# A scan layer and an MLP on one core: the state's part of y moved, PSUM banks named, the transposes of C and B taken apart

## The chip, the core and the metric

The kernel runs on one core of a Trainium2 chip. The metric is the device time of one execution in microseconds (us). The kernel before was run four times: 368.15, 368.38, 367.01 and 365.83 us, a median of 367.58. Engines are named as in the profile: PE (TensorE's matmuls), PEld (TensorE's weight loads), DVE (VectorE), ACT (ScalarE), POOL (GpSimd), and SP, whose queue issues all transfers.

## What is computed

Two layers, one after the other, for 4 batches, 8 heads, 768 tokens, head width D = 32, state width N = 16. The first is a scan in chunks (the reference takes chunks of 32 tokens; the result does not depend on the length):

```python
cum = np.cumsum(la, axis=-1)                      # la = log of the decay a, within a chunk
L = np.exp(cum[:, :, :, None] - cum[:, :, None, :]) * causal
M = np.einsum('bhin,bhjn->bhij', Cc, Bc) * L      # scores, decayed
y_intra = np.einsum('bhij,bhjd->bhid', M, xc)     # own products
y_inter = np.einsum('bhin,bhnd->bhid', Cc, state) * decay_to_i[:, :, :, None]
y[:, :, sl] = y_intra + y_inter
state = decay_full * state + np.sum(Bx, axis=2)
```

The second is an MLP on the 3072 tokens: `h = x @ w_in` (256 to 2048), `g = h * clip(h + 3, 0, 6) / 6`, `out = g @ w_out` (2048 to 256). The weights arrive as 64-bit floats, and DVE and ACT decode them to fp32 at the start.

## The kernel before

**Tiling.** The kernel works in NC = 6 chunks of 128 tokens, all 4 batches together, and each chunk in two halves of 64 tokens. Every engine's instructions stand in the order in which the code is written out by hand (`manual_schedule`); waits between engines follow from the tiles. Chunk c of the scan is computed while the MLP of chunk c - 1 runs; the main loop is over k, the MLP's chunk, with c = k + 1.

**The scan for a chunk.** `load_bc` and `load_x` bring C, B and x (L85, L112). The decays L come from `diff_mask`, `diff_less`, `diff_pick` and `diff_exp` for chunks 0 and 1 (L309 to L340: a bank is filled with a mask by one matmul, then sums of logs are added, then ACT takes exp), and by a transfer through DRAM with `conceal` and `decay` for later ones. `turn(c, p)` (L389) transposes C and B for two batches at a time on TensorE into one bank t_ps; ACT copies bT, and ACT or DVE make cT (C masked for odd and even heads) and csT (C times the decay from the chunk's start, eto). From chunk 3 on `turn_all` does this on DVE. `scores(c)` (L433) makes the products cb of B and C in four banks and the sums sp for the state in banks y0 and y1, then on DVE multiplies L by cb (L463) and forms mid, later and the new state (L469 to L485). `mix(c)` (L492) then makes y in four banks: one blank product (L503), the state's products for both halves (L510; mid for second halves, the last chunk's state for first halves), then the own products (L519). `keep` copies y to SBUF as yT by four ACT copies, `sum_y` forms differences of its quarters.

**The MLP.** For k = 0, `mlp_in` (L534) makes each of 16 blocks h by plain products into bank tag "f", ACT takes the ramp, DVE multiplies (L618), and the decoding of the weights is woven between (`weights(i, n)` takes n more steps of part i; parts 0 to 3 are w_in, 4 to 7 are w_out). `first_out` makes the output, and between its calls the scan of chunk 1 is called: turn, scores, results. For k >= 1, both products run by a scheme with seven half products in place of eight: `lead`, `early`, `middle` and `last` (L582 to L609) for 8 steps s, `out_units` (L676) for the output; in it, scores(c) stands at unit 2 and results(c), which is mix, keep and sum_y, at unit 6. For k = 1 the calls turn(2, 0) and turn(2, 1) stand at steps 3 and 5.

**Banks.** PSUM has 8 banks: pool ps with four buffers under the one tag "f", taken in turn, ps_o with two, and ps_y with y0 and y1.

**The start.** Before the first h: masks for chunks 0 and 1, logs and their sums, diff for chunk 0, decoding of part 0, diff for chunk 1, eto, `ends` (POOL: B times decay), turn(0, 0) and turn(0, 1), scores(0), mix(0), `by_token` (four transposes into c_ps, L300, and one DVE step), keep(0), and the rest of part 1:

```python
diff_exp(1, 2)
diff_exp(1, 3)
weights(1, 1)
scores(0)
ys = mix(0)
by_token()
keep(0, ys)
weights(1, 4)
```

Of the kernel before, what the change touches and what calls it, by code (L numbers as in the profile page):

```python
# [20 lines left out]
def kernel(  # L21
# [45 lines left out]
    ps = ctx.enter_context(tc.tile_pool(name="ps", bufs=4, space=PSUM))  # L67
# [229 lines left out]
    def by_token():  # L297
        c_ps = ps.tile([P, NC, G], FP32, name="c_ps", tag="f")
        for c in range(2, NC):
            nc.tensor.transpose(out=c_ps[:, c], in_=cum_c[:, c], identity=ident[:G, :G])  # L300
        nc.vector.tensor_scalar(
            out=cum_n[:, 2:], in0=c_ps[:, 2:], scalar1=-1.0, scalar2=None, op0=ALU.mult)


    yTs, states, mids, bTs, bss, tmps = {}, {}, {}, {}, {}, {}

    ds = {}

    def diff_mask(c, b):  # L309

        if c == 0:
            d = ps.tile([P, NH, HT], FP32, name="d", tag="f")
        elif b < 2:
            d = ps_o.tile([P, NH, HT], FP32, name="d", tag="o")
        else:
            d = ps_y.tile([P, NH, HT], FP32, name="d", tag=f"y{b % 2}")
        nc.tensor.matmul(
            out=d, lhsT=ident_h, rhs=hide.unsqueeze(1).to_broadcast([P, NH, HT]),
            start=True, stop=True)
        ds[c, b] = d  # L320
# [21 lines left out]
    def first_eto():  # L342

        e_ps = ps.tile([P, NB, HT], FP32, name="e_ps", tag="f")
        for b in range(NB):
            nc.tensor.matmul(
                out=e_ps[:, b],
                lhsT=picks[:, b * P:(b + 1) * P],
                rhs=split[:, 0, HALF[1]], start=(b == 0), stop=True, skip_group_check=True)
        etos[0] = att.tile([P, NB, P], FP32, name="eto")  # L350
        nc.scalar.activation(etos[0][:, :, HALF[1]], e_ps, AF.Exp)
# [37 lines left out]
    def turn(c, p):  # L389


        bT, cT, csT = turned(c)
        bs_ = slice(2 * p, 2 * p + 2)
        pool, tag = (ps, "f") if c < 2 else (ps_o, "o")
        t_ps = pool.tile([P, 4, P], FP32, name="t_ps", tag=tag)
        for k in range(4):
            j, b = k // 2, 2 * p + k % 2
            nc.tensor.transpose(  # L398
                out=t_ps[:, k],
                in_=bcs[c][j][:, b * NH:(b + 1) * NH].rearrange("s h n -> s (h n)"),  # L400
                identity=ident)
        nc.scalar.copy(out=bT[:, bs_], in_=t_ps[:, 2:4])
        if c == 1 and p == 0:
            from_start(c)
            carry(c)
            for b in range(NB):
                ends(c, b)
        if c == 1 or (c, p) == (0, 1):
            for t in range(2):
                nc.scalar.activation(  # L410
                    cT[:, bs_, t], t_ps[:, 0:2], AF.Copy, scale=parity[:, t:t + 1])
        else:
            nc.vector.tensor_tensor(
                out=cT[:, bs_], in0=t_ps[:, 0:2].unsqueeze(2).to_broadcast([P, 2, 2, P]),
                in1=parity.unsqueeze(1).unsqueeze(3).to_broadcast([P, 2, 2, P]), op=ALU.mult)
        sl = slice(0, P) if c else HALF[1]
        nc.vector.tensor_tensor(
            out=csT[:, bs_, sl], in0=t_ps[:, 0:2, sl], in1=etos[c][:, bs_, sl], op=ALU.mult)
# [13 lines left out]

    def scores(c):  # L433


        bT, cT, _ = bTs[c]
        L, xt, bs = Ls[c], xts[c], bss[c]
        cbs = [ps.tile([P, NB, 2, HT], FP32, name="cb", tag="f") for q in range(NQ)]
        for b in range(NB):
            for a, rows in enumerate(HALF):  # L440
                for q in range(NQ):
                    pair = slice(32 * q, 32 * q + 32)

                    nc.tensor.matmul(  # L444
                        out=cbs[q][rows, b], lhsT=bT[pair, b, rows], rhs=cT[pair, b, :, rows],
                        start=(b == 0), stop=True, tile_position=(32 * q, a * HT),
                        skip_group_check=True)
        halves = range(2 if c < NC - 1 else 1)
        sps = [ps_y.tile([P, NB, 2 * D], FP32, name=f"sp{a}", tag=f"y{a}") for a in halves]
        for b in range(NB):  # L450
            for q in range(NQ):
                hs = slice(b * NH + 2 * q, b * NH + 2 * q + 2)
                for a in halves:
                    nc.tensor.matmul(  # L454
                        out=sps[a][32 * q:32 * q + 32, b],
                        lhsT=bs[HALF[a], hs].rearrange("s h n -> s (h n)"),
                        rhs=xt[HALF[a], hs].rearrange("s h d -> s (h d)"),
                        start=True, stop=True, tile_position=(a * HT, 32 * q),
                        skip_group_check=True)

        def pair_decayed(q):
            hs = slice(2 * q, 2 * q + 2)
            nc.vector.tensor_tensor(  # L463
                out=L[:, :, hs], in0=L[:, :, hs], in1=cbs[q], op=ALU.mult)

        def new_state(t, sp, old):
            for u in range(2):
                ds_ = slice(u * D, (u + 1) * D)
                nc.vector.scalar_tensor_tensor(  # L469
                    out=t[:, :, ds_], in0=sp[:, :, ds_], scalar=parity[:, u:u + 1],  # L470
                    in1=old[:, :, ds_], op0=ALU.mult, op1=ALU.add)

        pair_decayed(0)
        mids[c] = mid = att.tile([P, NB, 2 * D], FP32, name="mid", bufs=1)
        if c:
            new_state(mid, sps[0], tmps[c])
        else:
            nc.vector.tensor_tensor(
                out=mid.rearrange("p b (t d) -> p b t d", t=2),
                in0=sps[0].rearrange("p b (t d) -> p b t d", t=2),  # L480
                in1=parity.unsqueeze(1).unsqueeze(3).to_broadcast([P, NB, 2, D]), op=ALU.mult)
        if c < NC - 1:
            states[c] = att.tile([P, NB, 2 * D], FP32, name="state")
            later = att.tile([P, NB, 2 * D], FP32, name="later", bufs=1)
            nc.vector.tensor_tensor(  # L485
                out=later, in0=mid, in1=etos[c][:, :, P - 1:P].to_broadcast([P, NB, 2 * D]),
                op=ALU.mult)
            new_state(states[c], sps[1], later)
        for q in range(1, NQ):
            pair_decayed(q)  # L490

    def mix(c):  # L492

        xt, csT = xts[c], bTs[c][2]
        ys = {(a, 0): ps_y.tile([P, NB, HT], FP32, name=f"y{a}", tag=f"y{a}") for a in range(2)}
        for a in range(2):
            y2 = ps.tile([P, 2, NB, HT], FP32, name="y2", tag="f")
            ys[a, 1] = y2[:, 0]  # L500


        nc.tensor.matmul(  # L503
            out=y2[:, 1], lhsT=ident_h, rhs=hide.unsqueeze(1).to_broadcast([P, NB, HT]),
            start=True, stop=True, skip_group_check=True)
        for b in range(NB):
            for a in range(0 if c else 1, 2):
                for q in range(NQ):
                    pair, d0, u = slice(32 * q, 32 * q + 32), 2 * D * (q % 2), q // 2
                    nc.tensor.matmul(  # L510
                        out=ys[a, u][d0:d0 + 2 * D, b],
                        lhsT=(mids[c] if a else states[c - 1])[pair, b],
                        rhs=csT[pair, b, HALF[a]], start=(b == 0 and (a, u) != (1, 1)),
                        stop=True, tile_position=(32 * q, d0), skip_group_check=True)
        for b in range(NB):
            for h in range(NH):
                for a, rows in enumerate(HALF):
                    d0 = D * (h % HU)
                    nc.tensor.matmul(  # L519
                        out=ys[a, h // HU][d0:d0 + D, b], lhsT=xt[rows, b * NH + h],  # L520
                        rhs=Ls[c][rows, b, h], start=(c + a + b == 0), stop=True,
                        tile_position=(a * HT, d0), skip_group_check=True)
        return ys

    def keep(c, ys):

        yTs[c] = att.tile([P, NK, NB, P], FP32, name="yT")
        for (a, u), y in ys.items():
            nc.scalar.copy(out=yTs[c][:, u, :, HALF[a]], in_=y)
# [4 lines left out]
    def mlp_in(k, f):  # L534
        h = ps.tile([P, NK, 2 * P], FP32, name="h", tag="f")
# [46 lines left out]
    def lead(k, s):  # L582
# [3 lines left out]
        pool, tag = (ps, "f") if s % 3 == 2 else (ps_y, f"y{s % 3}")  # L586
        odds[k, s] = odd = pool.tile([P, 2, 2 * P], FP32, name="odd", tag=tag)
        evens[k, s] = even = ps.tile([P, 2, 2 * P], FP32, name="even", tag="f")
# [158 lines left out]
    def results(c):  # L747
        keep(c, mix(c))
# [17 lines left out]
    for c in range(2):  # L766
        for b in range(NB):
            diff_mask(c, b)
# [6 lines left out]
    for part in (diff_less, diff_pick):  # L775
        for b in range(NB):
            part(0, b)
# [9 lines left out]
    weights(0, 2)  # L787
    store_rows()
    for part in (diff_less, diff_pick):
        for b in range(NB):  # L790
            part(1, b)
    first_eto()
    for b in range(NB):
        ends(0, b)
    turn(0, 0)
    turn(0, 1)
    diff_exp(1, 2)
    diff_exp(1, 3)
    weights(1, 1)
    scores(0)  # L800
    ys = mix(0)
    by_token()
    keep(0, ys)
    weights(1, 4)
# [9 lines left out]
    for k in range(NC):  # L814
        gTs[k] = ffn.tile([P, NF, TB], FP32, name="gT")
        c, ahead = k + 1, k + 2
        if k == 0:
# [11 lines left out]
            for i in range(NP):  # L829
                for b in range(NB):  # L830
# [8 lines left out]
                    elif (i, b) == (2, 0):  # L839
                        turn(c, 0)  # L840
                        turn(c, 1)
                        for p in range(2):
                            conceal(ahead, p)
                    elif (i, b) == (2, 1):
                        scores(c)
                        next(sums_in)
# [40 lines left out]
        for i, _ in enumerate(out_units(k)):  # L887
# [8 lines left out]
            if c < NC:  # L896
                if i == 2:
                    scores(c)
                if ahead < NC and 2 <= i < 6:
# [41 lines left out]
```

## Time and profile before

| what | value |
|---|---|
| median of four runs | 367.58 us (365.83 to 368.38) |
| profiled execution, its own time | 368.15 us |
| its span, first to last instruction | 366.4 us |
| its mean granted clock | 0.991 |
| DVE, ACT, POOL busy | 61%, 48%, 37% |
| bytes moved | 24.95 MB, mean 68 GB/s |

The page's first part gives each engine's busy time and its share of the span. The second cuts the span into 40 slices of 9.16 us; a digit is tenths busy, and in the row PEclk tenths of TensorE's full clock. The third lists the transfer queues with packets, MB and share. The fourth follows the chain that ended last back from the end. In the chain in order of time a piece has its start and its length in us, the engine, the tile it writes and the line; "issue" is time in which an engine waited for nothing that the profile shows. In a list of waits a line says who waited for whom: total us, how often, and the longest.

Fp32 products take two passes, so the profile counts twice as many matmuls as the code has (L510 and L519 in chunk 4: 64 and 128, with as many weight loads).

### The profile page before, as it was taken

The page shows a single profiled execution, that of the slowest core. Times are in us where ns is not written, and L with a number is a line of the kernel's source. Part 1 is how long each engine was busy: PE and PEld are TensorE (multiplying, and loading weights), DVE is VectorE, ACT ScalarE, POOL GpSimd, SP SyncE. Part 2 cuts the span into 40 slices and gives each one's busy share as a digit, 9 for nine tenths or more (in the row PEclk, how much of TensorE's full clock was granted, in tenths as well). Part 3 has the DMA queues.
Part 4 walks back from the last instruction along what each step waited for, and adds up shares of the span by engine and source line. Part 5 has one row for each costly group of instructions (what it writes and reads, how often), then busy time and mean ns, then how long its engine had stood idle before and what let it go on. Part 6 is the DMA issues. An engine that isn't in the chain of part 4 may idle for free.

```text
span 366.4 us, 9281 instructions
## 1 busy us (share of the span) xinstructions
PE 351.3 (96%) x3910; PEld 301.0 (82%) x3910; DVE 225.0 (61%) x429; ACT 175.5 (48%) x389; POOL 137.4 (37%) x138
## 2 busy tenths in 40 slices
PE   6769999999999989999989999999999999999996
PEld 2544448878788989888989888999888999888996
DVE  7558999876588616588517488436488412488111
ACT  4738878447575730476640366550366110367100
POOL 3300000172299812069803059910057800058800
PEclk9969999999999999999999999999999999999999
DMA  9967979900936016460007442000000000000000
GB/s 168 168 269 168 124 267 144 161 2 32 184 46 87 4 31 147 73 93 8 2 4 174 65 83 27 2 4 30 29 0 3 2 4 30 30 1 2 0 30 29
DMA packets 78537, 24.95 MB, mean 68 GB/s; under 512 B 69088, under 2 KB 74880, under 8 KB 77984
## 3 DMA queue, kind: packets, MB, share of 16 engines
q1 hardware_dynamic: 78496, 24.37, 35.6%
q8 instruction: 30, 0.49, 0.6%
q14 instruction: 11, 0.09, 0.1%
HBM read 21.07 MB, written 3.29 MB: 66 GB/s over the span
## 4 chain that ended last, share of the span: by engine, by line
PE 93%; DVE 3%; issue 1%; DMA 1%; ACT 1%; DVEq 0%; ACTq 0%
PE even L579 19%; PE ob L688 18%; PE oa L688 17%; PE odd L579 14%; PE h L537 8%; PE o L629 7%; PE y L519 3%; PE cb L444 2%; PE y L510 1%; PE sp L454 1%; PE d L323 1%; PE d L332 1%; DMA out_dram<-ob 1%; PE t_ps L398 1%; DMA pre<-in_a_dram 1%
## 5 line engine op out<-in xcount | busy, mean ns | idle before, releaser
L674 POOL TENSOR_TENSOR s<-gT 128x512 f32<-128x512 f32 x20 | 26.4, 1320 | 88.0 <-DVE gT L618 88.0
L579 PE MATMUL even<-ts,w_sum 128*128 128x256 f32 x160 | 48.2, 383 | 0.0
L592 ACT COPY even<-odd 128x512 f32<-128x512 f32 x40 | 23.0, 575 | 47.1 <-PE odd L579 44.9
L613 ACT ACTIVATE gT<-odd,half 128x512 f32<-128x512 f32 x40 | 27.5, 687 | 35.1 <-DVE odd L606 35.1
L579 PE MATMUL odd<-yT,w_in 128*128 128x256 f32 x160 | 41.1, 379 | 0.0
L688 PE MATMUL oa<-w_out,gT 128*128 128x128 f32 x320 | 38.9, 277 | 0.0
L688 PEld LDWEIGHTS oa<-w_out,gT 128*128 128x128 f32 x320 | 38.1, 192 | 0.9
L688 PE MATMUL ob<-w_out,s 128*128 128x128 f32 x320 | 37.4, 275 | 0.0
L688 PEld LDWEIGHTS ob<-w_out,s 128*128 128x128 f32 x320 | 36.5, 192 | 0.0
L579 PEld LDWEIGHTS even<-ts,w_sum 128*128 128x128 f32 x160 | 29.9, 190 | 5.3 <-ACT up L599 1.5
L618 DVE SCALAR_TENSOR_TENSOR gT<-gT,odd 128x512 f32<-128x512 f32 x40 | 27.5, 688 | 9.8 <-ACT gT L613 9.7
L579 PEld LDWEIGHTS odd<-yT,w_in 128*128 128x128 f32 x160 | 30.1, 190 | 3.9
L360 ACT ACTIVATE L<-L,cum_n 128x64 f32<-128x64 f32 x128 | 31.2, 340 | 2.8 <-POOL L L153 2.8
L378 POOL TENSOR_TENSOR tmp<-state,eto 128x256 f32<-128x256 f32 x5 | 3.3, 653 | 74.3 <-DVE w_in L561 56.4
L688 PE MATMUL ob<-t,gT 128*128 128x128 f32 x240 | 30.3, 279 | 0.1
L593 DVE COPY up<-odd 128x256 f32<-128x256 f32 x40 | 17.0, 424 | 21.3 <-ACT even L592 17.4
L618 DVE SCALAR_TENSOR_TENSOR gT<-gT,even 128x512 f32<-128x512 f32 x40 | 27.2, 679 | 4.4 <-ACT gT L613 4.4
L613 ACT ACTIVATE gT<-even,half 128x512 f32<-128x512 f32 x40 | 27.7, 693 | 4.4 <-PE even L579 4.4
L537 PE MATMUL h<-yT,w_in 128*128 128x512 f32 x64 | 29.0, 615 | 0.0
L688 PEld LDWEIGHTS ob<-t,gT 128*128 128x128 f32 x240 | 27.9, 192 | 1.2 <-issue 0.4
L629 PE MATMUL o<-w_out,gT 128*128 128x256 f32 x128 | 28.7, 381 | 0.0
L629 PEld LDWEIGHTS o<-w_out,gT 128*128 128x128 f32 x128 | 24.1, 190 | 3.7 <-issue 0.5
(126 smaller groups left out, 632.7 us busy)
## 6 DMA issues: line engine op xcount, KB each, us to landing
raw<-in_moe_w_in_dram SPq DMA_DIRECT2D x4, 1024.0 KB
raw<-in_moe_w_out_dram SPq DMA_DIRECT2D x4, 1024.0 KB
L<-cum_d SPq DMA_DIRECT2D x8, 512.0 KB
xt<-in_x_dram SPq DMA_DIRECT2D x6, 512.0 KB
out_dram<-res SPq DMA_DIRECT2D x20, 128.0 KB
B<-in_B_dram SPq DMA_DIRECT2D x6, 256.0 KB
eto<-cum_e SPq DMA_DIRECT2D x20, 64.0 KB
C<-in_C_dram SPq DMA_DIRECT2D x3, 256.0 KB
```

The lines of the kernel that those rows point to most:

```text
L360: nc.scalar.activation(Ls[c][:, b, h], Ls[c][:, b, h], AF.Exp, bias=cum_n[:, c, g:g + 1])
L444: nc.tensor.matmul(out=cbs[q][rows, b], lhsT=bT[pair, b, rows], rhs=cT[pair, b, :, rows], start=(b == 0), stop=True, tile_position=(32 * q ...
L519: nc.tensor.matmul(out=ys[a, h // HU][d0:d0 + D, b], lhsT=xt[rows, b * NH + h], rhs=Ls[c][rows, b, h], start=(c + a + b == 0), stop=True, ...
L537: nc.tensor.matmul(out=h.rearrange("p r i -> p (r i)"), lhsT=w_in[:, j, f * P:(f + 1) * P], rhs=yTs[k][:, j].rearrange("p b i -> p (b i)") ...
L579: nc.tensor.matmul(out=bank[:, r], lhsT=lhsT, rhs=rhs, start=start, stop=True, skip_group_check=True)
L592: nc.scalar.copy(out=even, in_=odd[:, 1:2].to_broadcast([P, 2, 2 * P]))
L593: nc.vector.tensor_copy(out=up[:, 1], in_=odd[:, 0])
L613: nc.scalar.activation(gTs[k][:, f], h.rearrange("p r i -> p (r i)"), AF.Relu, bias=half, scale=1.0 / 6.0)
L618: nc.vector.scalar_tensor_tensor(out=g, in0=g, scalar=1.0, in1=h.rearrange("p r i -> p (r i)"), op0=ALU.min, op1=ALU.mult)
L629: nc.tensor.matmul(out=o[:, b % 2], lhsT=gTs[0][:, f, b * P:(b + 1) * P], rhs=w_out[:, f], start=(f == 0 and b % 2 == 0), stop=True, skip_ ...
L674: nc.gpsimd.tensor_tensor(out=o, in0=p_, in1=q_, op=op)
L688: nc.tensor.matmul(out=bank[:, slot], lhsT=lhs[:, j], rhs=rhs[:, j], start=(clear and j == 0), stop=True, skip_group_check=True)
```

## The change

State's products are taken out of `mix` into `from_state(c, a)`. For first halves (a = 0) it is called inside `scores`, ahead of cb; for second halves (a = 1) at the end of `mix`, behind the own products, which now run bank by bank (u outermost). Banks y0 and y1 each hold a set of first halves' y and a set of sp side by side; second halves' y take f0 and f1. The blank product is gone.

DVE's part of `scores` becomes `multiply` (two products of L and cb, mid, two products) and `renew` (later and state), and ACT first copies the second half's sp to SBUF as `adds`, also for the last chunk. For chunk 0 renew(0) stands inside part 1's decoding, and two of keep(0)'s four copies are DVE's. The last chunk computes both sets of sp.

Every bank of ps has a tag of its own, f0 to f3. `mlp_in` takes f0 to f3 in turn, `lead` takes f0 and f2, f1 and f3, or y0 and y1 by s % 3.

`turn(c, j)` turns B (j = 1) or C (j = 0) of all four batches; cT and csT are then 128x512 at once. For chunk 1 B is turned first, then come `wake` (exp of eto, carry, ends) and C. For chunk 2, C is turned at step 3 and B at step 5.

At the start the mask and diff for chunk 1's batches are split: (2, 3) ahead of the transposes, 1 behind them, 0 between scores(0) and mix(0). C's transposes and cT stand ahead of the last step of part 0's decoding, and the first step of part 1 moves from ahead of scores(0) to behind keep(0).

```diff
-    ps = ctx.enter_context(tc.tile_pool(name="ps", bufs=4, space=PSUM))
+    ps = ctx.enter_context(tc.tile_pool(name="ps", bufs=1, space=PSUM))
...
+    def turn_c(c, t_ps):
+        transposes(c, 0, t_ps)
+        cT = turned(c)[1]
+        for t in range(2):
+            if c == 1:
+                nc.scalar.activation(cT[:, :, t], t_ps, AF.Copy, scale=parity[:, t:t + 1])
+            else:
+                nc.vector.tensor_scalar(
+                    out=cT[:, :, t], in0=t_ps, scalar1=parity[:, t:t + 1], scalar2=None,
+                    op0=ALU.mult)
...
+    def from_state(c, a):
+        csT, state = bTs[c][2], (mids[c] if a else states[c - 1])
+        for b in range(NB):
+            for q in range(NQ):
+                pair, d0 = slice(32 * q, 32 * q + 32), 2 * D * (q % 2)
+                nc.tensor.matmul(
+                    out=ys[c][a, q // 2][d0:d0 + 2 * D, b], lhsT=state[pair, b],
+                    rhs=csT[pair, b, HALF[a]], start=(a == 0 and b == 0), stop=True,
+                    tile_position=(32 * q, d0), skip_group_check=True)
...
     def scores(c):
+        both = [ps_y.tile([P, 2, NB, HT], FP32, name=f"y{u}", tag=f"y{u}") for u in range(2)]
+        ys[c] = {(0, u): both[u][:, 0] for u in range(2)}
+        sps[c] = [both[a][:, 1] for a in range(2)]
+        if c:
+            from_state(c, 0)
...
-        halves = range(2 if c < NC - 1 else 1)
...
+    def multiply(c):
+        adds[c] = att.tile([P, NB, 2 * D], FP32, name="adds", bufs=1)
+        nc.scalar.copy(out=adds[c], in_=sps[c][1])
...
     def mix(c):
-        nc.tensor.matmul(
-            out=y2[:, 1], lhsT=ident_h, rhs=hide.unsqueeze(1).to_broadcast([P, NB, HT]),
-            start=True, stop=True, skip_group_check=True)
...
+        for u in range(2):
+            for b in range(NB):
+                for h in range(u * HU, (u + 1) * HU):
+                    for a, rows in enumerate(HALF):
...
+        from_state(c, 1)
...
-    weights(0, 2)
+    weights(0, 1)
     store_rows()
-    for part in (diff_less, diff_pick):
-        for b in range(NB):
-            part(1, b)
     first_eto()
+    diff(1, 2, 3)
     for b in range(NB):
         ends(0, b)
-    turn(0, 0)
-    turn(0, 1)
+    turn_c(0, t_ps)
+    weights(0, 1)
+    turn_b(0)
+    fade_c(0, t_ps)
     diff_exp(1, 2)
     diff_exp(1, 3)
-    weights(1, 1)
+    diff(1, 1)
     scores(0)
-    ys = mix(0)
+    diff_mask(1, 0)
+    diff(1, 0)
+    multiply(0)
+    mix(0)
     by_token()
-    keep(0, ys)
-    weights(1, 4)
+    keep(0)
+    weights(1, 2)
+    renew(0)
+    weights(1, 3)
...
                     elif (i, b) == (2, 0):
+                        turn(c, 1)
+                        wake(c)
                         turn(c, 0)
-                        turn(c, 1)
...
                     elif (i, b) == (2, 1):
                         scores(c)
+                        multiply(c)
+                        renew(c)
...
                 if i == 2:
                     scores(c)
+                    multiply(c)
+                    if c < NC - 1:
+                        renew(c)
```

## The prediction

> **What bounds the kernel now.** I read the page's busy table, its clock row and the chain by engine first, then the chain in order of time, last the waits of TensorE.
>
> ```profile
> PE 351.3 (96%) x3910; PEld 301.0 (82%) x3910; DVE 225.0 (61%) x429; ACT 175.5 (48%) x389; POOL 137.4 (37%) x138
> PEclk9969999999999999999999999999999999999999
> q8 instruction: 30, 0.49, 0.6%
> PE 93%; DVE 3%; issue 1%; DMA 1%; ACT 1%; DVEq 0%; ACTq 0%
> ```
>
> TensorE is the path: 93% of the chain, and no other engine is near. A gain must shorten TensorE's work or close one of its few gaps. The clock row has one dip, near 22 to 28 us. The chain in order of time shows the gaps (start us, us, what):
>
> ```profile
> 15.31 0.69 DVE cT L413
> 16.04 1.55 PE cb L444 x59
> 17.59 0.83 PE sp L454 x53
> ...
> 18.86 0.44 DVE later L485
> 19.41 0.61 DVE state L469 x2
> 20.02 1.80 DVE L L463 x3
> 21.86 0.44 PE y L519 x8
> 22.30 1.60 issue
> 23.89 1.61 PE y L519 x92
> 25.50 0.56 PE c_ps L300 x4
> ...
> 73.69 0.44 DVE csT L417
> ...
> 132.06 1.15 PE y L519 x75
> 133.21 1.18 issue
> 134.39 0.43 PE y L519 x25
> ```
>
> TensorE's own list of waits adds that the same kind of gap comes three times:
>
> ```profile
> PE y L519 <- issue: 3.9, 3, 1.6
> PE cb L444 <- DVE cT L413: 1.9, 1, 1.9
> PE y L510 <- DVE state L469: 1.5, 1, 1.5
> PE cb L444 <- DVE csT L417: 0.6, 1, 0.6
> ```
>
> So: 1.9 us at 14.1 to 16.0 (cT), 1.5 at 18.7 to 20.2 (VectorE's mid, later and state before y), and three "issue" gaps inside y, 1.60 at 22.30, 1.18 at 133.21 and 1.13 at 189.26.
>
> **What the "issue" gaps are.** I counted TensorE's instructions in the built program (a weight load and a matmul each count, fp32 products twice): 7,855. The three gaps stand before instructions 708, 3012 and 4292, which are all 196 plus a multiple of 256. Queue q8 moved 30 packets of 16 KB, 256 instructions of 64 bytes each. So a gap is TensorE at the edge of a block of code that has not come. In the packet times a fetch begins 1.1 to 1.6 us after an edge has been crossed out of a stall (25.07 after 23.89; 135.98 after 134.39; 191.50 after 190.40), less where TensorE's sequencer had run ahead; it takes about 1.0, and the gaps end 1.2 to 1.5 after it landed. A block run through faster than about 3.4 us from that crossing stalls. Only scores and mix run so fast: L510's 128 instructions take 1.09 us and L519's 256 take 1.45 (chunk 4).
>
> [...]
>
> **The change, part by part.** In the changed program, counted the same way (7,915 instructions), the edges at 196 + 256n fall elsewhere. I assume the same offset.
>
> *Chunks 1 to 5, mix.* The blank product L503 goes: 0.11 us of chain each time ("130.86 0.11 PE y L503"), 5 x 0.11 = 0.55 saved; in chunk 0 it lay under a wait. State's 16 products for first halves (64 instructions, half of L510's 1.09, so 0.55 us) move ahead of the scores: work unchanged, but the dense runs become 320 and 320 instructions, where they were 256 and 386. They need csT and the last state, which are old by then, except in chunk 1. Own products now run by bank, L546, same count and tiles; the nearest row is L519's 1.45 us and I keep it. VectorE's order (two products, mid, two products, then later and state) ends far ahead of mix: scores end at 123.5, mix starts at 130.9, and all of it is 4 to 5 us. ACT's added copy (128x256, 0.37 by L402) is hidden: ACT is 48% busy and waits 33.6 us for y.
>
> *Edges in those chunks.* Chunk 2: edges at 2756, 21 instructions into own products, and 3012, 19 into state's last ones: one dense block of 1.50 us. The nearest fetches, whose edge lay 3 and 29 instructions into mix (5316 and 6596), began 0.45 us before it was executed; so 0.45 ahead, 1.0 fetch, 1.35 to use is 1.9 us, a gap of 0.4 (0 to 0.8) where 1.18 was: saves 0.8. Chunk 3: edges at 4036 (16 instructions before mix ends its wait in the output units) and 4292 (239 into L546): 3.2 us apart with the sequencer ahead: no gap, saves 1.13. Chunk 4: none before, none after. Chunk 5: L519 took 1.68 where 1.45 is clean; the edge moves into the units: saves 0.25. Together 2.2.
>
> *Chunk 1.* B is turned first, then eto's exp, then C. ScalarE's chain is bT at 128x512 (L592's row, 0.575), eto 0.63, two cT at 128x512 (0.6 each), VectorE's csT 0.69 by the 128x512 products: from 70.85 to 74.0. TensorE has 8 output products to 73.15 and now cannot begin scores at all without csT (before, a few cb ran ahead of a 0.57 us wait): 0.85 us idle, 0.3 lost. Bounds: 0 if ScalarE overlaps as it does before, 0.9 if each step is a tenth longer.
>
> *Chunk 2's turning.* In the loop of stage 1 VectorE gets two cT and csT of 128x512, 1.9 us in one step, where L413 and L417 took 1.1 in each of two. It works 2.7 of 3.0 us a step. up (106.15) and the sums behind it move 0.9 later, to end at 108.35; TensorE wants them for "last" at 108.23: 0.15 lost (0 to 0.5). The final chunk's second set of sp, 16 products more (L454 takes 0.79 with two sets, 0.58 with one): 0.21 lost.
>
> *Start.* Products of diff for chunk 1 shrink ahead of C's turning: e_ps 0.22, two less 0.86, half of L332's second run 0.6, so C's transposes at 11.9; B landed at 12.55. VectorE's two cT (0.69 each by the 128x512 rows) run 12.4 to 13.7, ahead of the 2.2 us of L211 and L219 that held them before; ScalarE's bT ends by 14.1; diff(1,1) ends by 13.9. So cb starts near 14.2 instead of 16.04 and ends 15.8; sp then waits for x, whose last packets landed at 16.24, so it ends near 17.2. VectorE: L211, L219, csT to 16.4, then products 0, 1, mid, 2, 3: 19.4. TensorE: diff(1,0) 1.2 us to 18.4, own products of the first bank to 19.1. Without another limit c_ps would end at 21.3.
>
> But edge 708 now lies 132 instructions into own products, at the second bank's start, and it needs the fetch raised at edge 452 (now 40 into sp, before 4 into it). Before, 452 was crossed at 17.5 and the packet began only at 21.57, when the second of three 1 MB weight loads had ended: q1 then moved 400 KB each us. The crossing comes at most 0.5 to 1 us sooner. Bounds: 17.5 (not held) to 24.1 (held to the third load's end). I take 21.2, just before the row, since the same loads stand in the queue. Then code at 23.5, the rest of own products 0.7, state's 16 products 0.5, c_ps 0.56: h starts at 25.3 instead of 26.06. Now the clock. The page's row dips because the granted clock is 0.5 from 21.76 to 28.59. [...] I take 0.4.
>
> Behind that start, decode of weight part 1 is put after keep: ScalarE's copy goes from 19.52 to about 25.2, and VectorE's yT copies, later and state add 2.1 us, so L219 ends near 32.0 (was 31.07). The first user, h's fifth block, starts at 33.6 (was 34.24): covered, with 1.6 us left, and VectorE's idle 0.75 and 0.62 us at 34.4 and 42.0 take up the delay. The next w_out load, which waits for L206, and what SP has queued behind it (eto, C, B, x) go about 1 us later; they are used from 44 and 70 on.
>
> **Sum.** -0.4 (start) -0.55 (L503) -2.2 (edges) +0.3 (chunk 1) +0.15 (turning) +0.21 (sp) = -2.5. On the profiled execution, 368.15 (span 366.4 and 1.75 around it): 365.65. It stands 0.57 above the median of the four, 367.58, so the forecast is 365.1.
>
> **Rivals.** (1) *The fetch is not held.* If it starts within 1.1 us of its crossing or after the first load (19.0), TensorE never idles long, h starts at 21.6 to 23.1 and the clock may stay full (1.3 more). VectorE then becomes the bound: its 2.1 us of added work make w_out's first part come 0.5 to 1.1 us after its use. Net 2.5 to 4.6 plus the 2.1 elsewhere: 361 to 363, say 361.8. For it: the other fetches after a stall began within 1.6 us. Against: the 4 us of this very one. 0.20.
> (2) *The edges do not move as counted* (another offset, or gaps bound to something else): 3.9 us of gaps stay, and 0.4 + 0.55 - 0.66 remains: 367.3. For it: offset and delay rest on three gaps. 0.17.
> (3) *Slower: the fetch is held to the end of the third load.* [...] Against: the third load stood behind this fetch before. 0.13.
> (0) *The forecast*, 365.1, 364 to 366.3. 0.50.
>
> What a measurement of this kernel tells from no change is about 0.5%, 1.84 us: faster is below 365.74. From (0) 0.36, (1) 0.20, (2) 0.02: 0.58. Same: 0.36. Slower, above 369.4, only from (3) or a turning that stalls every engine: 0.06. Range 361.5 to 367.7, leaving out half of (1) and most of (3).
>
> **What would show it.** Right: cb near 14.2; an "issue" gap of some 4 us at 19.5 to 23.5; gaps at chunk 3 gone, at chunk 2 below 0.8; no L503; TensorE idle about 0.85 before chunk 1's state products. Wrong: gaps at edges other than those counted, h before 23.5 or after 27, waits on VectorE in the stage of h or at 108 us above 0.5.

## The result

The changed kernel took 365.80 us (median of 32 runs, 364.70 to 367.27), the kernel before 367.67 (53 runs, 365.12 to 369.86): a ratio of 0.9953, 95% interval 0.9941 to 0.9965. That is 1.87 us between the medians. The interval lies wholly below 1; still, 365.80 is just short of the 365.74 (0.5%) below which the forecast would have called the kernel faster. 365.1 was forecast. The profiled execution of the changed kernel took 366.78 us. Its page, the same lines as before:

```profile
span 365.1 us, 9338 instructions
PE 349.8 (96%) x3936; PEld 300.3 (82%) x3936; DVE 223.5 (61%) x429; ACT 176.7 (48%) x386; POOL 137.8 (38%) x138
PEclk9978999999999999999999999999999999999999
q8 instruction: 31, 0.51, 0.6%
PE 86%; DVE 4%; DMA 3%; ACT 2%; issue 2%; SPq 2%; DVEq 0%; ACTq 0%
```

TensorE works 1.5 us less and the span is 1.3 shorter. TensorE's share of the chain fell from 93% to 86%, but that alone is no loss: a chain may run through another engine's work that ends just in time. TensorE's own list of waits says what it stood still for (the waits for `split` and for B, and one of 2.1 us for POOL, left out here, come before the first scores):

```profile
PE y L546 <- issue: 4.4, 1, 4.4
...
PE even L610 <- DVE odd L639: 1.2, 1, 1.2
PE y L493 <- DMA xt<-in_x_dram: 1.2, 1, 1.2
PE d L324 <- DVE split L263: 1.1, 1, 1.1
PE y L462 <- DVE csT L426: 0.9, 1, 0.9
PE t_ps L400 <- DMA B<-in_B_dram: 0.8, 1, 0.8
```

The wait for cT (1.9) and that for state (1.5) are gone; of three "issue" gaps one is left, and it has 4.4 us in place of 1.6. Two lines are as foretold, x for sp (1.2) and csT in chunk 1 (0.9). One was not in the forecast: `even` waits 1.2 us for `odd` (0.3 before). The chain in order of time (start us, us, what) shows where the long gap is and that chunk 2 has none:

```profile
16.38 0.85 PE y L493 x48
...
18.13 0.80 PE y L546 x54
18.93 4.38 issue
23.31 1.05 PE y L546 x63
24.36 1.06 PE y L462 x32
25.42 0.56 PE c_ps L300 x4
...
133.18 1.46 PE y L546 x99
134.64 0.62 PE y L462 x32
```

**Where the time went.** TensorE's milestones cut the two profiled executions into four stretches that add up to the whole (us; first product of each kind):

| stretch | before | changed | difference | forecast |
|---|---|---|---|---|
| start to the first output product of chunk 0's MLP | 54.84 | 55.67 | +0.83 | -0.4 |
| from there to its last (chunk 1's scan inside) | 35.12 | 34.99 | -0.13 | +0.2 |
| from there to the next chunk's output units | 25.53 | 26.68 | +1.15 | +0.15 |
| from there to the end (chunks 2 to 5) | 247.61 | 244.42 | -3.19 | -2.4 |
| sum | 363.10 | 361.76 | -1.34 | -2.5 |

The forecast's terms are put where they fall: L503 at 0.11 a chunk, sp's 0.21 in the last row. The first row is above the usual in this execution. Three other profiled kernels with the same start (the experiments on the buffers, on chunk 1's order and on chunk 1's added products) have their first output product at 54.67, 54.66 and 54.12, and the one other kernel with the start of before (its experiment on the buffers) at 55.21. By the means of these, the start gains about 0.25 and the sum is about -2.4, 0.5 more than the 1.9 between the medians; single executions stand here against medians, and the 0.5 is not explained.

### The profile page after: what moved, and what is told of

It is laid out like the page before. It is cut to its first block, busy times and chain, and to the rows that moved or that the text cites. A ratio compares the mean times of both kernels' runs of the same rounds, so it can differ in the third digit from the quotient of the medians.

```text
span 365.1 us, 9338 instructions
## 1 busy us (share of the span) xinstructions
PE 349.8 (96%) x3936; PEld 300.3 (82%) x3936; DVE 223.5 (61%) x429; ACT 176.7 (48%) x386; POOL 137.8 (38%) x138
## 4 chain that ended last, share of the span: by engine, by line
PE 86%; DVE 4%; DMA 3%; ACT 2%; issue 2%; SPq 2%; DVEq 0%; ACTq 0%
PE ob L721 18%; PE oa L721 17%; PE even L610 16%; PE odd L610 12%; PE h L568 8%; PE o L662 7%; PE y L546 2%; DMA xt<-in_x_dram 2%; PE y L462 2%; SPq L92 1%; PE cb L485 1%; PE y L493 1%; DMA out_dram<-ob 1%; DVE odd L639 1%; DVE up L626 1%
## 5 line engine op out<-in xcount | busy, mean ns | idle before, releaser
L626 DVE COPY up<-odd 128x256 f32<-128x256 f32 x40 | 17.0, 425 | 22.5 <-ACT even L625 17.6
L568 PE MATMUL h<-yT,w_in 128*128 128x512 f32 x64 | 29.9, 631 | 0.0
```

What stands on the lines that cost most here:

```text
L568: nc.tensor.matmul(out=h.rearrange("p r i -> p (r i)"), lhsT=w_in[:, j, f * P:(f + 1) * P], rhs=yTs[k][:, j].rearrange("p b i -> p (b i)") ...
L626: nc.vector.tensor_copy(out=up[:, 1], in_=odd[:, 0])
```

## The experiments

The theory: TensorE stalls at every 256th instruction whose code has not come; what the change gained is where those edges fall, the long stall at the start is a fetch held behind the weight loads, and the forecast missed one wait, `odd`. Rivals: the stalls are bound to something else in mix or scores; the moved products are worth something by themselves; the stall at the start is not the loads'. Ratios are to the kernel before, run beside each. Where products are added, they write what the next product overwrites; nothing is left out.

**Edges, without the change.** 32 bf16 products (64 instructions) ahead of chunk 0's scores, in the kernel before:

```diff
+        if c == 0:
+            for _ in range(32):
+                nc.tensor.matmul(
+                    out=cbs[0][HALF[0], 0, 0], lhsT=ident_h[:, HALF[0]], rhs=hide,
+                    start=True, stop=True, tile_position=(0, 0), skip_group_check=True)
         for b in range(NB):
```

> The kernel before, with 32 small bf16 products (64 instructions, overwritten by cb's first product) in TensorE's wait of 1.9 us ahead of scores(0). It adds no work to the path; it moves every later code edge 64 instructions up the program. Theory (gaps are blocks of code that come late): in mix the edges then lie at 15, 233, 195, 221 of chunks 2 to 5, so no dense block of 256 stands whole between two edges after a late crossing: the gaps of 1.18 and 1.13 us in chunks 2 and 3 vanish, chunk 0's stays and ends about 23.9. Ratio to before 0.994 (2.0 to 2.4 us faster). Rival (the gaps belong to the work in mix, a bank or a wait that the records do not show): both gaps stay and the time is the same, or 0.3 us longer.

Measured: 0.9977 (0.9958 to 0.9995), 366.92 us. That is 0.7 us, less than expected. The gaps of chunks 2 and 3 went: chunks 2 to 5 take 244.74 us for 247.61, 2.9 less, by the moved edges alone. But a new gap came ahead of c_ps, where none had been, the clock was at half from 22.67 to 32.91, and the first output product came 2.7 us later. In TensorE's waits:

```profile
PE c_ps L301 <- issue: 2.0, 1, 2.0
PE y L525 <- issue: 1.8, 1, 1.8
```

The new gap stands before instruction 964, which is 196 + 3 x 256. So the gaps belong to the count of instructions and not to mix: the rival of a wait inside y falls. The traces show the same without the count of the built program: in all 12 of the profiled kernels that stall at edge 708, before and changed, padded or not, the stall stands before TensorE's 350th traced matmul, and that of 964 exactly 128 matmuls (256 instructions) behind it.

**The same with 24 products** (48 instructions), counted so that 964 lies in h, where products are slow enough (all of h is 128 instructions in some 29 us):

> The kernel before with 24 small products in place of 32 in TensorE's wait ahead of scores(0), so that the edges go up by 48 instructions and not by 64. With 64 the edge at 964 fell on c_ps, close behind chunk 0's own products, and cost a new gap of 2.0 us. Theory: with 48 it falls into h, whose blocks take 15 us, so only chunk 0's one gap stays, those of chunks 2 and 3 are away, and the kernel before gains about 2 us: ratio 0.993 to 0.996, what the whole change gained. Rival (padding itself costs what it saves): 0.998, as with 64.

Measured: 0.9871 (0.9853 to 0.9890), 362.96 us: 4.7 us, more than expected. Chunks 2 and 3 have at most 0.3 us left, and the one gap at the start now ends at 22.21, where it ended at 23.89:

```profile
19.63 0.24 PE y L525 x8
19.87 2.34 issue
22.21 1.84 PE y L525 x116
24.05 0.56 PE c_ps L301 x4
24.62 5.61 PE h L543 x11
```

h starts 1.5 us sooner, `even` no longer waits for `odd`, and the clock is at half for 3.41 us (22.55 to 25.96) where it was for 6.83 (21.76 to 28.59). By stretches of the table above, 2.0 us came off the start, 0.7 off the way to the next chunk's output units and 2.5 off chunks 2 to 5. Idle products alone thus beat the whole change more than twice over.

**The held fetch, first try.** In the changed kernel, the loads of weight parts 1 to 3 behind a memset of POOL's (part 3's was issued by part 0's decoding; the line that turns that off is not shown):

```diff
         raw = loads.tile([P, NK * FP * 2 * P], U32, name="raw", bufs=NRAW)
+        if i == 1:
+            nc.gpsimd.memset(raw[:, 0:1], 0)
...
-    load_w(1)
-    load_w(2)
...
+    for i in (1, 2, 3):
+        load_w(i)
     turn_c(0, t_ps)
```

> The changed kernel, with the loads of weight parts 1, 2 and 3 issued only after POOL's first element of part 1's buffer is written, which stands behind the four bs (about 15.7), so that their packets begin near 17.5 and not at 15.3. Theory (chunk 0's code fetch is held behind those loads): the fetch starts near 17.6 in place of 20.87, the gap of 4.38 us at 18.9 falls below 1.5, h starts at 22 to 23 in place of 25.98. Of some 3.5 us, VectorE's later decoding takes 0.5 to 1 back in the stage of h. Ratio to before 0.987 to 0.99. Rival (the fetch is late for another reason): the gap stays at 4 us and the ratio at 0.995, or above it because part 1 lands later.

Measured: 0.9950 (0.9931 to 0.9968), 365.97 us: as the changed kernel. The loads began only 0.9 us later (16.38 for 15.50), just ahead of the crossing at 16.5, and the fetch began at 20.71 (20.87). The gate opened too early to test the theory. It does show that the fetch does not wait for the end of the second load: that came 0.9 us later (22.66 for 21.73), and the fetch did not.

**The held fetch, second try.** The same three loads behind ACT's copy `adds`, at 17.6 us:

```diff
+        if i == 1:
+            nc.scalar.copy(out=raw[:, 0:1].bitcast(FP32), in_=half)
...
     multiply(0)
+    for i in (1, 2, 3):
+        load_w(i)
     mix(0)
```

> The changed kernel, with the loads of weight parts 1 to 3 issued behind ScalarE's copy of sp, about 17.7, so that their packets begin near 19.4, two us after the code fetch of edge 452 is due (17.6). The first gate moved them only from 15.7 to 16.9 and changed nothing. Theory (the fetch waits behind the loads' packets on its engine): it starts before 18.5, the gap of 4.2 us at 18.9 falls below 1.5, h starts at 21.5 to 23. Part 1 lands near 22, so ScalarE's first copy and VectorE's decoding come 0.5 to 1 us later than h would allow, and part of the gain is lost in the stage of h. Ratio 0.987 to 0.991. Rival (such a fetch takes 4 us at this place whatever the loads do): gap and ratio stay at 4 us and 0.995.

Measured: 0.9884 (0.9865 to 0.9902), 363.35 us. In stretches of 1 us of this kernel (columns: stretch, its length, busy time of PE, PEld, DVE, ACT and POOL with instructions, granted clock, share of the engines that move data, GB/s), nearly nothing is moved at 17 to 18:

```profile
16.00:17.00 1.00, 0.64 (x64) 0.67 (x64) 1.00 (x3) 0.00 (x0) 0.00 (x0) 1.00 0.18 42
17.00:18.00 1.00, 1.00 (x40) 0.48 (x22) 1.00 (x3) 0.46 (x2) 0.00 (x0) 1.00 0.06 16
18.00:19.00 1.00, 0.92 (x73) 0.77 (x67) 0.91 (x2) 0.08 (x1) 0.00 (x0) 1.00 0.23 37
```

In the same table of the changed kernel the engines' share is 0.84 at 17 to 18, and then it is full:

```profile
18.00:19.00 1.00, 0.94 (x75) 0.79 (x68) 0.86 (x2) 0.06 (x1) 0.00 (x0) 1.00 1.03 414
19.00:20.00 1.00, 0.00 (x0) 0.00 (x0) 0.00 (x0) 0.32 (x1) 0.00 (x0) 1.00 0.99 406
```

The edge was crossed at the same time (16.46 and 16.48); the fetch began at 17.79 where it began at 20.87, the gap fell from 4.4 to 1.2, h started at 22.0 and the clock stayed at 1.00 until the last product's end. That h then waits for the decoding is the price, since the weights come later; TensorE's waits:

```profile
PE h L570 <- DVE gT L653: 1.2, 1, 1.2
PE y L548 <- issue: 1.2, 1, 1.2
...
PE even L612 <- DVE odd L641: 0.9, 1, 0.9
...
PE h L570 <- DVE w_in L221: 0.4, 1, 0.4
```

**The wait for odd.** `up` (L626) and the first stage's output tile share the tag "ob" of a pool, with two buffers, so a copy into `up` waits until the output has left. In the changed kernel's chain:

```profile
91.12 0.59 ACT ob L667
91.72 0.02 issue
91.73 3.47 DMA out_dram<-ob
...
95.32 0.42 DVE up L626
95.75 0.35 DVE odd L638
...
96.19 0.44 DVE odd L639
```

In the chain of the kernel before the same transfer is shorter:

```profile
91.03 2.92 DMA out_dram<-ob
```

Own buffers for the output tile, in the changed kernel (e3) and in the kernel before (e7):

```diff
-            ob = ffn.tile([P, 2, DM], FP32, name="ob", bufs=2)
+            ob = ffn.tile([P, 2, DM], FP32, name="ob", tag="first", bufs=2)
```

> The changed kernel, with buffers of their own for the first stage's output tile ob, so that the MLP's up does not wait for that tile's transfer. Theory: TensorE's gap of 1.2 to 1.6 us at 95 to 97 us (1.2 on VectorE's sums, which wait behind up for the transfer) closes: 0.8 to 1.4 us faster than the changed kernel, ratio to before 0.992. Rival: the gap is made up by the next wait in the loop (ScalarE's even), and the ratio stays 0.995.

> The kernel before with buffers of their own for the first stage's output tile, as e3 had on the changed kernel, where it gained 1.5 us. Theory (the changed kernel comes to the same wait with more to lose, since chunk 2's own gaps are gone and its code fetch runs into the transfer): here TensorE's gap is 0.3 us, so 0.2 to 0.5 us are gained, ratio 0.999. Rival (the wait costs both kernels the same): 1.5 us, ratio 0.996.

Measured: 0.9904 (0.9882 to 0.9925), 364.33 us, in the changed kernel, and 0.9978 (0.9956 to 1.0000), 367.07, in the kernel before. By the medians the wait cost the changed kernel about 1.5 us and the kernel before about 0.6, which alone would not be clear of no change. The profiles agree: the stretch to the next chunk's output units fell from 26.68 to 25.03 us and from 25.53 to 24.85. With both kernels freed of the wait, that leaves 0.18 for the turning at chunk 2.

**Why the transfer took longer.** A fetch of code lies on it: 92.30 to 93.73 in the changed kernel, 91.52 to 92.47 before, and 15 of the 16 signals of its landing were there by 93.88, the last at 95.20 (93.19 and 93.95 before). All profiled runs show it: in nine a fetch lies on this transfer, and the last signal comes 0.7 to 1.5 us behind the fifteenth, each time within 0.2 us of the fetch's own length; in the other four (before with 32, with 24 and with 24 products, gate and buffers; changed with 20 products) no fetch lies on it, and the last comes within 0.03 us. To move that fetch away, 20 products (40 instructions) in chunk 1 ahead of `from_state`, where TensorE waits for csT anyway:

```diff
+        if c == 1:
+            for _ in range(20):
+                nc.tensor.matmul(
+                    out=cbs[1][0][HALF[0], 0, 0], lhsT=ident_h[:, HALF[0]], rhs=hide,
+                    start=True, stop=True, tile_position=(0, 0), skip_group_check=True)
         if c:
             from_state(c, 0)
```

> The changed kernel with 20 products more (40 instructions, overwritten) in chunk 1, where TensorE waits for csT anyway; it moves every later edge 40 instructions towards the start. The fetch that lay on 92.30 to 93.73, on top of the first output's transfer (91.73 to 95.20), should then lie some 3 us sooner. Theory: that fetch delays one engine's share of the transfer, and with it up, odd and TensorE: TensorE's wait for odd falls from 1.2 to 0.3 to 0.6, the transfer's landing is back to 2.9 us or less, ratio 0.9925 to 0.9945. Rival: the transfer takes 3.5 us by itself and the wait stays at 1.0 or more: ratio 0.995 to 0.997. Chunk 2's edges fall 19 instructions ahead of own products and inside them; a gap of up to 0.5 may come there, which would show as issue before own products.

Measured: 0.9952 (0.9931 to 0.9972), 365.90 us, no gain, which misses the expected ratio; but the mechanism is there. The fetch came at 86.28, the second `up` began 2.3 us after the transfer was issued (3.6 in the changed kernel), and `even` no longer waits: the stretch to the next chunk's output units is 1.3 us shorter than the changed kernel's (25.35). But chunks 2 to 5 are 1.3 longer (245.68), at an edge in chunk 5; the expectation had looked at chunk 2 alone. TensorE's waits:

```profile
PE y L551 <- issue: 3.8, 1, 3.8
...
PE y L498 <- issue: 1.0, 1, 1.0
```

and the chain in chunk 5:

```profile
285.42 0.98 PE cb L490 x54
286.40 0.77 PE y L498 x52
287.17 1.05 issue
288.21 0.27 PE y L498 x2
```

Edge 6340 had moved into `from_state`, so that all of the scores' dense run stands between it and 6596.

**Chunk 1's order.** The state's products of chunk 1 behind cb, so that the wait for csT lies behind other work:

```diff
-        if c:
+        if c > 1:
             from_state(c, 0)
...
+        if c == 1:
+            from_state(c, 0)
```

> The changed kernel, with chunk 1's state products behind cb instead of ahead of it, all else the same. Theory (chunk 1's scores start 0.3 to 0.4 us late because they wait for csT): cb can run while csT is made, the wait of 0.9 us at 74 shrinks to 0.3 to 0.6, ratio 0.994, a gain at the edge of what can be told. Rival: cb waits for the same bank of C's transposes (csT reads it last), so nothing is gained: 0.995.

Measured: 0.9947 (0.9926 to 0.9967), 365.84 us, no difference from the changed kernel that can be told. cb waits 0.2 for cT and 0.3 for csT in place of one wait of 0.9.

**Together.** The changed kernel with the gate of the second try and the buffers:

> The changed kernel with the later loads of e6 and the buffers of e3. If both work and do not share their gain: the sum, ratio 0.982 to 0.987. If e6's gate does nothing: 0.990, as e3. If the later weights bind in the stage of h: above e3's 0.990.

Measured: 0.9844 (0.9824 to 0.9863), 361.96 us; the two gains add up. The kernel before with the 24 products, the gate and the buffers, and nothing of the change; the loads stand behind an ACT copy here:

```diff
     diff_exp(1, 3)
+    for i in (1, 2, 3):
+        load_w(i)
```

> The kernel before with 24 products of work that is overwritten, the loads of weight parts 1 to 3 behind a copy of ScalarE's at the end of diff for chunk 1, and a buffer of its own for the first stage's output tile; nothing of the change is in it. Theory: what the change gained lies in where the 256-instruction edges fall, not in moved work; then the 24 products keep their 4.7 us, the gate lets the fetch for edge 708 start near 18 (19.84 with the products alone) and takes up to 1.5 us more, the buffer 0.6: ratio to the kernel before 0.980 to 0.986, no issue gap above 1 us at the start. Rival: the order of the change is worth something of its own, 2 us or more, that this kernel lacks: ratio 0.988 or above, and slower than the changed kernel with gate and buffer (0.9844).

Measured: 0.9851 (0.9815 to 0.9887), 362.60 us. The fetch began at 18.27 and y does not stall; the next block's does, before instruction 964, with 1.1 us (`PE h L545 <- issue: 1.1, 1, 1.1`). By these six runs, of 360.84 to 363.88 us, it can't be told from the changed kernel with the same two aids; whether the order of the change is worth up to some 1.5 us either way stays open. Last, the changed kernel with gate and buffers, and renew(0) moved from the decoding into the loop over h, at its last block, since h waited for DVE:

```diff
-    weights(1, 2)
-    renew(0)
-    weights(1, 3)
+    weights(1, 5)
...
+                if f == NF - 1:
+                    renew(0)
```

> The changed kernel with gate and buffer, and renew(0), VectorE's 1.05 us of later and state, moved from inside the decoding of part 1 to the end of the loop over the blocks h. It tests what took the gate's gain in part: h then waited 1.2 us for gT and 0.4 for w_in. Theory: VectorE became the bound there, so 0.8 to 1.2 us come off: ratio 0.981 to 0.9825. Rival: the wait only moves to a later block, since VectorE's whole work in the stage is unchanged: ratio 0.984 within 0.001, with the same sum of waits of h for VectorE.

Measured: 0.9830 (0.9803 to 0.9858), 361.65 us, the fastest here. Its interval covers the 0.9844 from which it should differ. In the profile h's wait for gT fell from 1.2 to 0.8 us, that for w_in stayed 0.4, and the output products got one of 0.2: the start is 0.56 us shorter than with gate and buffers (51.60 for 52.16) and the next stretch 0.61 longer (35.67 for 35.06). So the wait moved on, as the rival has it, and whether anything was gained is open.

## Why the prediction held, point by point

**The gap at the start: right, its time in part by luck.** cb began at 13.98 (forecast 14.2), the fetch at 20.87 (21.2), the block ran at 23.31 (23.5). It stands before 708, as counted. That the loads hold the fetch was an assumption; the second gate shows it. But the forecast read "when the second load had ended" out of one row, and that is not what sets the time. The fetch began 0.9 us ahead of that end in the changed kernel (20.87, end 21.73), 2.0 ahead with the first gate and 1.5 ahead with 24 products. What the nine kernels without the second gate or its like share is the time from the crossing of 452 to the fetch, 3.3 to 4.4 us; 21.2 came out close because the crossing moved by 1.0 us only. The table has eight of the stalls; in those of the other runs, too, a block runs 2.3 to 2.9 us after its fetch began, whatever the fetch waited for.

| kernel, edge | edge before it crossed | fetch began | block ran |
|---|---|---|---|
| before, 708 | 17.53 | 21.57 | 23.89 |
| changed, 708 | 16.48 | 20.87 | 23.31 |
| before with 24 products, 708 | 15.70 | 19.84 | 22.21 |
| changed with second gate, 708 | 16.46 | 17.79 | 20.09 |
| before with 32 products, 964 | 22.64 | 24.32 | 26.65 |
| before, 3012 | 131.49 | 132.06 | 134.39 |
| before, 4292 | 187.44 | 187.50 | 190.40 |
| changed with 20 products, 6596 | 285.14 | 285.66 | 288.21 |

**How long it is held: only measured.** The first load ran from 15.5 to 19.2 in the changed kernel, the second to 21.7, the third to 25.9; the fetch began inside the second, 1.7 us after the first load's end. In the others it began 2.6 (before), 1.1 (24 products) and 0.6 us (first gate) after that end. So neither the first load's end nor the second's sets the time of the fetch by itself, and what does was not shown.

**The clock: what it costs lies in where its stretch falls.** Half clock lay at 23.52 to 30.35 in the changed kernel's profile, 6.83 us as before (21.76 to 28.59), but 4.4 us of h's run lay in it instead of 2.6, so the first output product came 0.83 late though h started 0.10 early. In the runs with the three other orders or buffers on the same start it ended at 28.44, 28.27 and 27.53, and 2.1 to 2.6 us of it lay in h. Over all nine profiles without the second gate or its like, the time from h's first product to the first output product is 27.54 to 27.64 us and half of what of it ran at half clock (0.50, by the granted clock). So the size of the loss is where the stretch of half clock happens to lie; the row before, with its end at 28.59, is that of one execution. No run shows the forecast's 0.4 for the start, which the author had estimated; in its place the means show 0.25 gained, and the one execution 0.83 lost.

**Edges: right, and larger.** Forecast 2.2 us, of it 0.4 of chunk 2's gap left over. Chunk 2's gap is gone whole (1.18), because the fetch began 0.76 us ahead of the edge's execution and not 0.45; chunk 3's 1.13 is gone, and chunk 5's own products take 1.44 for 1.68. Chunks 2 to 5 gained 3.19 in all where 2.4 were forecast. The rest of the surplus lies in the two chunks that had gaps (1.46 and 1.43 us saved, of which 1.29 and 1.24 are gap and L503). These stalls cost more than their gaps, since the products next to them ran slow: in chunk 2 L519 took 1.15 and 0.43 us beside the gap, for 1.45 without one. The kernel before with 32 products, which has nothing else of the change, saved 1.40 and 1.36 in these two chunks. Its 2.9 in all four, with L503 (-0.44) and sp (+0.21), make 3.1 of the 3.19. Chunks 4 and 5 saved 0.13 and 0.17, as forecast (0.11 and 0.15).

**Chunk 1: wrong by 0.3.** The wait for csT is 0.9 us, as foretold (0.85), but the stretch is 0.13 shorter instead of 0.2 longer. The step that failed is the 0.3 charged as the difference of two waits, for the wait before was read too small. The list gives it 0.57 us, but from 73.08 on only six products of cb had run before the rest could start at 74.17 (this view of before ends at 75 us):

```profile
73.08 0.51 PE L444 MATMUL cb<-cT,bT 32*64 32x128 f32 x6
74.17 1.08 PE L444 MATMUL cb<-cT,bT 32*64 32x128 f32 x54 [0.57 <-DVE csT L417]
```

cb ended at 75.32, 2.24 us after it began, where chunk 2's takes 1.14: its wait cost 1.1 us, and the changed kernel's 0.92. So nothing was lost there.

**Chunk 2's turning: right.** 0.15 forecast, 0.18 between the two kernels with buffers of their own (one profiled execution of each).

**The step that is missing: `odd`.** The sum has no term for the first output's transfer and for `up` behind it. The new count of instructions was read for stalls of TensorE alone, and not for the transfers on which the moved fetches fall. The wait grew by 0.9 us in the profile, and the experiments with buffers give the same difference (1.5 against 0.6). The run with 20 products shows that moving the fetch away takes the wait with it.

So -2.5 was forecast and -1.9 measured. In the profiles the edges gave about 0.8 more, chunk 1 0.3 more, and `odd` took 0.9 to 1.0; the start gained less than 0.4 by the means and lost 0.8 in the one execution. That the sum came out close is in part because these errors cancel. Rival (1), a fetch that is not held (361.8), and rival (3), held to the third load's end, did not come true; (1) can be had with the gate (363.35), and h then waits for DVE, as that rival said. Rival (2), edges that do not move as counted, did not come true either: the gaps came and went where the count put them.

## What to carry to other kernels

If TensorE "waits for issue" in a dense run of small products, count its instructions: if the gaps lie a multiple of 256 apart, as here (before 708, 3012 and 4292, and before 964 with products added), the order of the work is not at fault, and a few products more or fewer ahead of it move every later edge, for better and for worse (here -4.7 us with 48 instructions and -0.7 with 64). A change that adds or removes instructions should be compared with the kernel before at a good shift of its own, or the shift is credited to the idea: here the two reach 0.985 and 0.984 with the same aids. And look at which tiles share a tag of a pool: one that is still being sent away can hold up work that has nothing to do with it.

## What was not expected of the hardware

- With a 16 KB fetch of code on top of a 256 KB transfer, the last of the 16 signals of its landing came behind the fifteenth by about the fetch's own length: 1.3 us where the fetch took 1.43, and 0.76 in the kernel before, where it took 0.95.
- Two fetches whose edges were crossed at 16.46 and 16.48 began 1.3 and 4.4 us later, one beside transfers at 6% of their engines in the us after the crossing and one beside transfers at 84% and then at all of them.
- In the nine kernels without the second gate or its like, chunk 0's transposes of B began between 12.68 and 14.01 us, and the clock was at half for 3.41, 6.83, 10.24 or 13.66 us. Whether that makes the spread of 4.7 us between runs of the kernel before was not tried.
